# Two fused attention layers on one core: full-bank score pieces, halved output transposes of the last batch, chunk-major x, and a new table of task order

## The chip, the cores and the metric

One core of a Trainium2 chip runs the whole program in one launch. The metric is the device time of that core in microseconds (us), the median of three runs. The engines named below are TensorE (PE, with its weight-load queue PEld), VectorE (DVE), ScalarE (ACT), GpSimd (POOL) and SyncE (SP, which only issues transfers). They run side by side and wait for each other through semaphores.

## The reference

The first layer is a linear attention without softmax, with a norm over each head; the second is a mixture of four small attention experts, two of which count for each token.

```
kv  = einsum('bhsd,bhse->bhde', k, v)          # b=8, h=8, s=576, d=e=64
out = einsum('bhsd,bhde->bhse', q, kv)
x   = out / sqrt(mean(out*out, -1) + 1e-6) * g_norm      # -> (8, 576, 512)

logits = x @ w_gate                             # 4 experts, the best 2 kept
w      = softmax over the 2 kept logits
for e in range(4):
    q, k, v = x @ wq[e], x @ wk[e], x @ wv[e]   # 64 wide each
    a  = softmax(causal(q @ k.T / 8))           # 576 x 576
    y += (w of e, 0 where not kept) * (a @ v @ wo[e])
```

## The kernel before

The work is cut by batch `b` (8 of them), and a batch's 576 tokens by tiles of 128, 128, 128, 128 and 64. The function `graph` lists every piece of work as a task (`("kv", b, c)`, `("x", b, i)` and so on) with its engine, an assumed duration, what it needs and which buffers it holds. The function `plan` walks through these tasks once while the program is built, and takes at each point the ready task with the lowest number from `urgency`, which is worked out from the tables `URGENCY`, `EDGES` and `PERIOD`. The instructions are then emitted in that order, so each engine has a fixed order, and a waiting instruction holds up all that stand behind it on its engine. `SWAP` and `ON_ACT` say whether a PSUM copy runs on ACT or on DVE. `COLD` is the planned time up to which PE's tasks are assumed to take 1.8 times as long.

The stages of a batch, with the task names in brackets:

- SP loads k, v and q. PE forms `p_kv` = k^T v for each head (L567), and copies put it into `kvx` and `kvc` (L454, L456); `p_kt` (L601) and `p_kg` (L611) turn it into four more columns that give the gate logits.
- q is turned by PE for batches 0 and 1 (`p_q`, L585) and by DVE for later ones. `p_out` (L630) is q times `kvx`, five tiles; its copy is `o_sb`, of which there is one buffer.
- ACT squares `o_sb` (L650), DVE sums by head (L656) and takes an inverse root in eleven small steps (L668 to L685).
- POOL multiplies `o_sb` by it and writes `x_tok` (task `xm`, L709), PE turns `x_tok` by four 128-wide transposes a tile (`p_x`, L585), and a copy makes `xT`. The weights' rows are laid out so that chunk `c` of x is every fourth column of `x_tok`.
- PE projects v (L770), q and k (L788) for the four experts, two by two (a pair). Before that POOL multiplies the weights by `g_norm` (task `ws`, L546), out of the same six `x` buffers that `x_tok` uses.
- The scores of a pair (`p_sc`, L814) are made in five pieces (`PIECES`), each in one two-bank PSUM buffer, one bank for each expert of the pair; ACT takes exp of a piece (L828), POOL sets the upper triangle to zero (L834), and PE multiplies by v (`p_pv`, L848).
- DVE scales the result to `osc` (L865 to L876), PE turns it (`p_ot`, L886), a copy makes `OT`, PE multiplies by wo (`p_y`, L896), and SP stores `y`.

PSUM is split into two one-bank buffers (`sm`) and three two-bank buffers (`bg`). The two places in the code that the change of layout and of pieces touches are, before:

```
t = tiles["x", b, i][:].rearrange("p h d -> p (h d)")
transpose_in(i, lambda c: t[:, c : c + NCH * (P - 1) + 1 : NCH], "x", b, i)
...
PIECES = (((0, 0, HALF),), ((0, HALF, S),), ((1, P, S),), ((2, 2 * P, S),), ((3, 3 * P, S), (4, 4 * P, S)))
```

Of the kernel before, what the change touches and what calls it, by code (L numbers as in the profile page):

```python
# [40 lines left out]
def graph(B):  # L41
# [14 lines left out]
    def copy(name, on_act, on_dve, needs, tiles=()):  # L56

        if engine_of(name) == "ACT":
            act(name, on_act, needs, tiles)
        else:  # L60
            dve(name, on_dve, needs, tiles)
# [4 lines left out]
    R5, R4, R2 = range(NB), range(NCH), range(EP)
    for b in range(B):
# [85 lines left out]
        for p in R2:  # L153
            for nm in "qk":
                pe((nm + "p", b, p), 1.12, xT + [("ws", nm, p)], (("bg", nm, b, p),))
            copy(("qpc", b, p), 0.64, 0.78, [("qp", b, p)], (("bg", "q", b, p), ("qTp", b, p)))
            copy(("kpc", b, p), 1.24, 1.50, [("kp", b, p)] + [("sc", b - 1, p, j) for j in R5], (("bg", "k", b, p),))
            hold = (0.31, 0.31, 0.46, 0.34, 0.46)
            took = (0.66, 0.66, 0.95, 0.72, 0.60)
# [2 lines left out]
            for j in R5:
                pe(("sc", b, p, j), hold[j], [("qpc", b, p), ("kpc", b, p)], (("bg", "sc", b, p, j), ("qTp", b, p)))
                act(("exp", b, p, j), took[j], [("sc", b, p, j)] + old, (("bg", "sc", b, p, j),))
                if j != 1:
                    pool(("msk", b, p, j), 0.41 if j < 4 else 0.70, [("exp", b, p, j)])
# [784 lines left out]
```

## Time and profile before

| | |
|---|---|
| median of three runs | 261.76 us (261.53 to 261.89) |
| profiled execution | 259.49 us |
| span of its trace, first to last instruction | 257.8 us |
| mean granted clock of TensorE in it | 0.934 of full speed |
| busy share of the span | PE 89%, PEld 80%, DVE 66%, ACT 59%, POOL 32% |

The profiled execution is one run, and 2.27 us below the median of the timed ones; 1.7 us of it lie outside the span. A busy share is an average over the whole span. In the rows further down, a granted clock of 1.00 is TensorE's upper level (2.4 GHz), and 0.50 its lower one (1.2 GHz).

### The profile page before, as it was taken

Reading aid. Unit: us, or ns where it says so; the run is one execution under the profiler, and the core shown is the slowest. Engines: PE = TensorE matmul, PEld = TensorE weight load, DVE = VectorE, ACT = ScalarE, POOL = GpSimd, SP = SyncE. Lnnn points to the kernel's source line nnn. Section 1 sums busy time; section 2 is a strip of 40 time slices with the busy share of each in tenths; the row PEclk is TensorE's granted clock in tenths of the full one; section 3 lists DMA queues with packets and bytes.
Section 4 is the critical chain, followed back from the end, with each engine's and each line's share of the span. In section 5 each row is a group of like instructions: output and inputs, shape, how many; then the busy total and the mean of one; then the engine's idle time right before and its main releaser. Section 6 shows DMA issues by size and latency. Waiting matters only on the chain.

```text
span 257.8 us, 6403 instructions
## 1 busy us (share of the span) xinstructions
PE 228.5 (89%) x2456; PEld 205.5 (80%) x2456; DVE 169.7 (66%) x503; ACT 152.5 (59%) x277; POOL 82.6 (32%) x160
## 2 busy tenths in 40 slices
PE   0726928999999999999999999989999999999963
PEld 0625826899999989998889889978998999989840
DVE  0085383317986785898688968865858889754560
ACT  0010622176967396449654985699657757976932
POOL 8201725000390038003720183018302730840500
PEclk9977775589999999999999999999999999999995
DMA  6998999999999379999898594131120202123045
GB/s 177 297 160 261 292 222 273 185 145 316 130 163 313 47 143 250 279 155 250 253 140 262 176 188 75 43 122 59 39 88 4 64 0 85 41 65 122 17 170 183
DMA packets 99432, 40.28 MB, mean 156 GB/s; under 512 B 76618, under 2 KB 94538, under 8 KB 99402
## 3 DMA queue, kind: packets, MB, share of 16 engines
q1 hardware_dynamic: 94320, 38.15, 64.0%
q10 hardware_dynamic: 5082, 1.72, 3.0%
q8 instruction: 19, 0.31, 0.6%
q14 instruction: 11, 0.09, 0.1%
HBM read 30.43 MB, written 9.44 MB: 155 GB/s over the span
## 4 chain that ended last, share of the span: by engine, by line
PE 78%; DMA 7%; DVE 6%; ACT 4%; SPq 1%; issue 1%; POOL 0%; DVEq 0%; POOLq 0%; ACTq 0%
PE p_out L630 15%; PE p_sc L814 9%; PE p_x L585 8%; PE p_q L788 7%; PE p_kv L567 7%; PE p_y L896 7%; PE p_v L770 7%; PE p_k L788 7%; PE p_pv L848 5%; DMA q_b<-in_q_dram 3%; DMA k_b<-in_k_dram 3%; ACT PT L828 2%; PE p_ot L886 2%; DMA w_stage<-in_moe_wv_dram 2%; PE p_kg L611 1%
## 5 line engine op out<-in xcount | busy, mean ns | idle before, releaser
L834 POOL TENSOR_SCALAR_AFFINE_SELECT PT<-PT 128x256 bf16<-128x256 bf16 (+1 forms) x80 | 29.3, 384 | 126.1 <-ACT PT L828 125.0
L828 ACT ACTIVATE PT<-p_sc 128x512 bf16<-128x512 f32 (+3 forms) x80 | 50.6, 718 | 3.4 <-PE p_sc L814 3.0
L709 POOL TENSOR_TENSOR x_tok<-o_sb,rs 128x512 f32<-128x512 f32 (+1 forms) x40 | 41.2, 1049 | 19.1 <-DVE rs L685 19.0
L630 PE MATMUL p_out<-kvx,qT 128*128 128x136 f32 x320 | 44.8, 290 | 0.9 <-DVE kvx L456 0.4
L630 PEld LDWEIGHTS p_out<-kvx,qT 128*128 128x128 f32 x320 | 41.2, 197 | 2.3 <-DVE o_sb L456 0.6
L814 PE MATMUL p_sc<-qTp,kT 128*128 128x288 f32 (+4 forms) x192 | 39.0, 323 | 0.0
L656 DVE TENSOR_REDUCE ms<-sq 128x8 f32<-128x520 f32 (+1 forms) x40 | 27.1, 687 | 17.7 <-ACT sq L650 17.2
L585 PE MATMUL p_x<-ident_f,x_tok 128*128 128x128 f32 (+1 forms) x160 | 28.3, 307 | 5.2 <-POOL x_tok L709 4.1
L650 ACT ACTIVATE sq<-o_sb 128x512 f32<-128x512 f32 (+1 forms) x40 | 25.0, 634 | 11.8 <-DVE o_sb L456 9.6
L814 PEld LDWEIGHTS p_sc<-qTp,kT 128*128 128x128 f32 x192 | 28.5, 190 | 3.6 <-ACT PT L828 0.7
L567 PE MATMUL p_kv<-v_b,k_b 128*64 128x64 f32 x512 | 23.4, 242 | 8.9 <-DMA k_b<-in_k_dram 7.8
L567 PEld LDWEIGHTS p_kv<-v_b,k_b 128*64 128x64 f32 x512 | 20.0, 153 | 12.4 <-issue 11.0
L456 DVE COPY o_sb<-p_out 128x544 f32<-128x544 f32 (+1 forms) x30 | 21.4, 716 | 11.2 <-PE p_out L630 11.0
L585 PEld LDWEIGHTS p_x<-ident_f,x_tok 128*128 128x128 f32 (+1 forms) x160 | 23.1, 209 | 7.1 <-POOL x_tok L709 5.5
L770 PE MATMUL p_v<-wv_r,xT 128*128 128x256 f32 x160 | 25.7, 292 | 0.7 <-DVE vext L456 0.7
L896 PE MATMUL p_y<-wo_b,OT 128*128 128x512 bf16 x80 | 23.8, 400 | 1.0 <-ACT OT L454 0.7
L454 ACT CAST kT<-p_k 64x576 fp32r<-64x576 f32 x32 | 20.3, 634 | 4.7 <-PE p_k L788 4.2
L770 PEld LDWEIGHTS p_v<-wv_r,xT 128*128 128x128 f32 x160 | 21.6, 189 | 1.6 <-DVE vext L456 1.1
L788 PE MATMUL p_q<-xT,wq_r 128*128 128x288 f32 x128 | 21.9, 323 | 0.0
L454 ACT CAST xT<-p_x 128x512 fp32r<-128x512 f32 (+1 forms) x25 | 13.3, 545 | 14.3 <-PE p_x L585 14.2
L788 PE MATMUL p_k<-xT,wk_r 128*128 128x288 f32 x128 | 20.2, 303 | 0.0
L788 PEld LDWEIGHTS p_q<-xT,wq_r 128*128 128x128 f32 x128 | 19.3, 206 | 0.3
(86 smaller groups left out, 319.1 us busy)
## 6 DMA issues: line engine op xcount, KB each, us to landing
out_dram<-y SPq DMA_DIRECT2D x32, 256.0 KB, 2.0
k_b<-in_k_dram SPq DMA_DIRECT2D x14, 512.0 KB, 5.2
v_b<-in_v_dram SPq DMA_DIRECT2D x14, 512.0 KB, 7.8
q_b<-in_q_dram SPq DMA_DIRECT2D x48, 144.0 KB, 4.2
q_b<-in_q_dram SPq DMA_DIRECT2D x6, 256.0 KB, 7.5
k_rem<-in_k_dram SPq DMA_DIRECT2D x8, 128.0 KB, 4.3
v_b<-in_v_dram ACTq DMA_DIRECT2D x4, 256.0 KB, 5.3
k_b<-in_k_dram SPq DMA_DIRECT2D x4, 256.0 KB, 6.7
```

What stands on the lines that cost most here:

```text
L454: nc.scalar.copy(dst, src)
L567: nc.tensor.matmul(p_kv[hh * Dh : (hh + 1) * Dh, c, :], lhsT=lhs, rhs=rhs, start=(j == 0), stop=(j == NF), skip_group_check=True,)
L585: nc.tensor.transpose(p_t[:, c, :nt], chunk(c)[:nt], ident_f[:nt, :nt])
L630: nc.tensor.matmul(p_o[:, c // 2, (c % 2) * 256 : (c % 2) * 256 + 2 * GW], lhsT=blocks_of(qT, c)[:, i * P : (i + 1) * P], rhs=kvx[b % 2][: ...
L656: nc.vector.tensor_reduce(mss[b % 2][:nt, i, :], sqs[(NB * b + i) % 3][:nt], axis=AX_X, op=AluOpType.add)
L709: nc.gpsimd.tensor_tensor(out=buf(("x", b, i), [P, H, Dh], FP32, "x_tok")[:nt], in0=ob[:nt, i, :, 0:Dh], in1=st["rstd", b][:nt, i * H : (i ...
L770: nc.tensor.matmul(p_v[:], lhsT=blocks_of(xTs[b % 2], c)[:, i * P : (i + 1) * P], rhs=w_r["v"][:, c, :, :].rearrange("p e f -> p (e f)"), ...
L788: nc.tensor.matmul(p_p[:, s, 0:HALF], lhsT=w_r[nm][:, c, 2 * pr : 2 * pr + 2, :].rearrange("p e f -> p (e f)"), rhs=blocks_of(xTs[b % 2], ...
L814: nc.tensor.matmul(p_s[:, el, o : o + hi - lo], lhsT=kTs[pr][el][:, kb * P : (kb + 1) * P], rhs=tiles["qTp", b, pr][:, lo:hi], start=True, ...
L828: nc.scalar.activation(PT[:, :, d0 : d0 + o], big("sc", b, pr, j)[:, :, 0:o], ACTF.Exp, scale=scale)
L834: nc.gpsimd.affine_select(out=d, in_=d, compare_op=AluOpType.is_ge, fill=0.0, base=0, pattern=[[0, 2], [1, w]], channel_multiplier=-1,)
L896: nc.tensor.matmul(p_y[:], lhsT=blocks_of(OTs[b % 2], pr)[:, qc * P : (qc + 1) * P], rhs=wo_b[:, pr, :], start=(pr == 0), stop=(pr == EP - 1),
```

## The change

1. The scores of a pair are made in four pieces in place of five. The first three hold 512 columns for each expert, which is a full bank, and the fourth holds 64. The matmuls of a pair stay twelve, and their columns stay the same in sum; there is one exp less.
2. `xm` writes `x_tok` with each chunk's 128 columns side by side, so that a transpose reads neighbouring values. The multiplication on POOL then writes four values 512 bytes apart before it goes on to the next four.
3. `p_ot` and its copy are cut in two for the last batch (three tiles, two tiles), and `p_y` of a tile waits only for its half.
4. Which engine does a PSUM copy is chosen task by task, and two of the six `ws` multiplications go from POOL to DVE.
5. `URGENCY`, `EDGES`, `PERIOD` and `COLD` have new numbers, so the order on every engine changes. The function `keep_warm`, which could put idle matmuls on PE, emits none, since `WARM` is 0.

```diff
-ON_ACT = ("kvc", "xc", "qpc", "kpc", "otc", "yc")
-SWAP = {"kgc": (6,), "ktc": (1,), "kvc": (0,), "kvx": (1,), "oc": (0, 1), "otc": (1,), ...
+SWAP = {
+    "ws": (('q', 0), ('v', 0),), "qc": ((0, 4), (1, 0), (1, 1), (1, 3),),
...
+    "kvc": ((1,),), "ktc": ((7,),),
+}
...
-    def copy(kind, b, dst, src):
-        if engine_of((kind, b)) == "ACT":
+    def copy(task, dst, src):
+        if tasks[task][0] == "ACT":
...
-COLD = 15.005
+WARM = 0.0
+COLD = 6.005
-PERIOD = 173.5
+PERIOD = 171.6
...
     def xm(b, i):
         nt = blocks[i][1]
+        shape = [nt, H, Dh // NCH, NCH]
         nc.gpsimd.tensor_tensor(
-            out=buf(("x", b, i), [P, H, Dh], FP32, "x_tok")[:nt],
-            in0=ob[:nt, i, :, 0:Dh],
-            in1=st["rstd", b][:nt, i * H : (i + 1) * H].unsqueeze(2).to_broadcast([nt, H, Dh]),
+            out=buf(("x", b, i), [P, NCH, P], FP32, "x_tok")[:nt].rearrange("p c (h r) -> p h r c", h=H),
+            in0=ob[:nt, i, :, 0:Dh].rearrange("p h (r c) -> p h r c", c=NCH),
+            in1=st["rstd", b][:nt, i * H : (i + 1) * H].unsqueeze(2).unsqueeze(3).to_broadcast(shape),
             op=AluOpType.mult,
         )
     def x_tr(b, i):
-        t = tiles["x", b, i][:].rearrange("p h d -> p (h d)")
-        transpose_in(i, lambda c: t[:, c : c + NCH * (P - 1) + 1 : NCH], "x", b, i)
+        transpose_in(i, lambda c: tiles["x", b, i][:, c, :], "x", b, i)
...
-    PIECES = (((0, 0, HALF),), ((0, HALF, S),), ((1, P, S),), ((2, 2 * P, S),), ((3, 3 * P, S), (4, 4 * P, S)))
+    PIECES = (
+        ((0, 0, NF * P),), ((0, NF * P, S), (1, P, S)), ((2, 2 * P, S), (3, 3 * P, S)), ((4, 4 * P, S),),
+    )
...
-    def ot(b, pr):
-        p_t = small([P, NB * P], "ot", b, pr, dtype=BF16)
-        for qc in range(NB):
+    def ot_part(part):
+        qcs = range(NB) if part is None else GROUPS[part][1]
+        return qcs, qcs[0] * P, min(S, (qcs[-1] + 1) * P)
+
+    def ot(b, pr, part=None):
+        at = (b, pr) if part is None else (b, pr, part)
+        p_t = small([P, NB * P], "ot", *at, dtype=BF16)
+        for qc in ot_part(part)[0]:
```

On PE, the order around the first x transposes (rows 19 to 30 of the program before) was, with `p_kv` of `k_rem_83` and every `p_out` here those of batch 1, and `p_x` and `p_q` out of `xT` those of batch 0:

```order
L585 MATMUL p_x<-ident_f,x_tok 128x128 x8
L567 MATMUL p_kv<-v_b,k_b 64x64 x8
L567 MATMUL p_kv<-v_rem_85,k_rem_83 64x64 x2
L567 MATMUL p_kv<-v_b,k_b 64x64 x8
L567 MATMUL p_kv<-v_rem_85,k_rem_83 64x64 x2
L585 MATMUL p_x<-ident_f,x_tok 128x128 x4
L601 MATMUL p_kt<-ident_f,kvc_89 128x128 x2
L585 MATMUL p_x<-ident_f,x_tok 128x128 x4
L611 MATMUL p_kg<-wg_bd,kvT 128x16 x2
L585 MATMUL p_x<-ident_f,x_tok 128x64 x4
L585 MATMUL p_q<-ident_f,q_b 128x128 x4
L788 MATMUL p_q<-xT_108,wq_r 128x288 x16
```

After the change (rows 22 to 33, all of `p_kv` of batch 1 standing ahead of them) it is:

```order
L625 MATMUL p_q<-ident_f,q_b 128x128 x8
L641 MATMUL p_kt<-ident_f,kvc_89 128x128 x2
L625 MATMUL p_x<-ident_f,x_tok 128x128 x4
L651 MATMUL p_kg<-wg_bd,kvT 128x16 x2
L625 MATMUL p_x<-ident_f,x_tok 128x128 x4
L625 MATMUL p_q<-ident_f,q_b 128x128 x4
L670 MATMUL p_out<-kvx_87,qT 128x136 x4
L625 MATMUL p_x<-ident_f,x_tok 128x128 x4
L670 MATMUL p_out<-kvx_87,qT 128x136 x4
L625 MATMUL p_q<-ident_f,q_b 128x128 x4
L625 MATMUL p_x<-ident_f,x_tok 128x128 x4
L670 MATMUL p_out<-kvx_87,qT 128x136 x4
```

Two q tiles of batch 1 and the second half of its `p_kv` now stand ahead of the first `p_x`; `p_out` of batch 1 stands between the x transposes of batch 0, and the projections follow it, v first.

On SP, the loads after those of batch 0 were:

```order
L540 DMA w_stage<-in_moe_wq_dram 128x2x256 x2
L540 DMA w_stage<-in_moe_wk_dram 128x2x256 x2
L540 DMA w_stage<-in_moe_wv_dram 128x2x256 x2
L555 DMA wo_st<-in_moe_wo_dram 128x512 x2
L493 DMA k_rem_83<-in_k_dram 64x8x64
```

After the change they are:

```order
L593 DMA wo_st<-in_moe_wo_dram 128x512 x2
L530 DMA k_rem_83<-in_k_dram 64x8x64
L530 DMA v_rem_85<-in_v_dram 64x8x64
L518 DMA k_b<-in_k_dram 128x4x256
L518 DMA v_b<-in_v_dram 128x4x256
L518 DMA k_b<-in_k_dram 128x4x256
L518 DMA v_b<-in_v_dram 128x4x256
L542 DMA q_b<-in_q_dram 128x8x64 x4
L542 DMA q_b<-in_q_dram 64x8x64
L577 DMA w_stage<-in_moe_wv_dram 128x2x256 x2
L577 DMA w_stage<-in_moe_wk_dram 128x2x256 x2
```

Six weight loads went behind the k, v and q of batch 1 (the two of wq further still, behind the k and v of batch 2).

On POOL, after the constants, the first rows were:

```order
L546 TENSOR_TENSOR wq_r<-w_stage,g_rows 128x2x4x64 x2
L546 TENSOR_TENSOR wk_r<-w_stage,g_rows 128x2x4x64 x2
L546 TENSOR_TENSOR wv_r<-w_stage,g_rows 128x2x4x64 x2
L709 TENSOR_TENSOR x_tok<-o_sb,rs 128x512 x4
L709 TENSOR_TENSOR x_tok<-o_sb,rs 64x512
```

After the change:

```order
L751 TENSOR_TENSOR x_tok<-o_sb,rs 128x128x4 x4
L584 TENSOR_TENSOR wv_r<-w_stage,g_rows 128x2x4x64
L584 TENSOR_TENSOR wk_r<-w_stage,g_rows 128x2x4x64 x2
L751 TENSOR_TENSOR x_tok<-o_sb,rs 64x128x4
L584 TENSOR_TENSOR wq_r<-w_stage,g_rows 128x2x4x64
```

The weights' multiplications stand behind four of the five `xm` of batch 0, and the fifth behind three of them.

## Rows read from the trace of the kernel before

**Rows 1.** Page, part 1: busy us, share of the span, instructions.

```profile
PE 228.5 (89%) x2456; PEld 205.5 (80%) x2456; DVE 169.7 (66%) x503; ACT 152.5 (59%) x277; POOL 82.6 (32%) x160
```

**Rows 2.** Windows: stretch, busy of PE, PEld, DVE, ACT, POOL, clock, DMA share, GB/s.

```profile
25.80:29.20 3.40, 3.40 (x17) 3.40 (x17) 1.08 (x2) 1.85 (x3) 3.40 (x4) 0.50 1.20 243
29.20:36.05 6.85, 3.82 (x61) 3.51 (x60) 4.45 (x13) 3.71 (x7) 1.70 (x2) 1.00 1.07 284
36.05:53.12 17.07, 13.65 (x87) 11.85 (x88) 6.34 (x24) 2.92 (x7) 5.09 (x5) 0.50 1.05 219
66.00:240.00 174.00, 172.28 (x1909) 157.89 (x1909) 134.80 (x406) 123.11 (x224) 61.08 (x106) 1.00 0.57 130
251.10:257.80 6.70, 2.59 (x6) 0.58 (x5) 0.00 (x0) 2.09 (x4) 0.00 (x0) 0.50 0.50 176
```

**Rows 3.** Waits of PE: total us, times, longest.

```profile
PE p_kv L567 <- DMA k_b<-in_k_dram: 7.8, 2, 7.4
PE p_q L585 <- DVE qT L456: 4.1, 2, 3.7
```

**Rows 4.** Timeline of PE: start, us, what, and the wait ahead of it.

```profile
32.73 0.69 PE L567 MATMUL p_kv<-v_b,k_b 128*64 128x64 f32 x16 [1.09 <-DMA v_b<-in_v_dram]
...
38.19 1.13 PE L585 MATMUL p_x<-ident_f,x_tok 128*128 128x128 f32 x4 [4.08 <-POOL x_tok L709]
```

**Rows 5.** Chain that ended last, 33 to 60 us: start, us, what.

```profile
37.05 1.09 POOL x_tok L709
...
49.29 3.84 PE p_q L788 x16
...
54.06 0.93 PE p_out L630 x8
...
55.82 3.90 PE p_out L630 x32
```

**Rows 6.** The same chain from 160 us on: projections at clock 1.00.

```profile
163.42 2.12 PE p_q L788 x16
```

**Rows 7.** Timeline of SP's issues: start, us, what.

```profile
14.03 3.50 SPq L540 DMA_DIRECT2D w_stage<-in_moe_wq_dram  x2
...
27.49 9.95 SPq L505 DMA_DIRECT2D q_b<-in_q_dram  x5
```

**Rows 8.** Weight loads of transposes of one tile each, at clock 1.00.

```profile
54.71 0.47 PEld L585 LDWEIGHTS p_q<-ident_f,q_b 128*128 128x128 f32 x4
...
55.35 0.32 PEld L585 LDWEIGHTS p_q<-ident_f,q_b 64*128 64x128 f32 x4 [0.17 <-issue]
...
153.43 0.56 PEld L585 LDWEIGHTS p_x<-ident_f,x_tok 128*128 128x128 f32 x4
...
160.33 0.55 PEld L585 LDWEIGHTS p_x<-ident_f,x_tok 64*128 64x128 f32 x4
```

**Rows 9.** Lines by form, POOL: count, busy us, mean ns, idle before.

```profile
L709 POOL TENSOR_TENSOR x_tok<-o_sb,rs 128x512 f32<-128x512 f32 x32 | 33.2, 1052 | 19.1 <-DVE rs L685 19.0
```

**Rows 10.** Lines by form, PE, two of the score matmuls.

```profile
L814 PE MATMUL p_sc<-qTp,kT 128*128 128x288 f32 x64 | 14.6, 325 | 0.0
...
L814 PE MATMUL p_sc<-qTp,kT 128*128 128x64 f32 x32 | 5.2, 246 | 0.0
```

**Rows 11.** Lines by form, ACT, the exps.

```profile
L828 ACT ACTIVATE PT<-p_sc 128x576 bf16<-128x576 f32 x32 | 20.0, 671 | 0.3 <-PE p_sc L814 0.3
L828 ACT ACTIVATE PT<-p_sc 128x896 bf16<-128x896 f32 x16 | 14.9, 932 | 1.0 <-PE p_sc L814 0.8 <-POOL PT L834 0.2
L828 ACT ACTIVATE PT<-p_sc 128x640 bf16<-128x640 f32 x16 | 11.4, 712 | 0.9 <-PE p_sc L814 0.9
L828 ACT ACTIVATE PT<-p_sc 128x512 bf16<-128x512 f32 x16 | 9.7, 605 | 1.2 <-PE p_sc L814 1.1
```

**Rows 12.** Timelines of the tail: DVE, then ACT.

```profile
246.60 0.68 DVE L456 COPY y<-p_y 128x512 f32<-128x512 f32 x1
...
249.04 0.64 ACT L454 COPY OT<-p_ot 128x576 bf16<-128x576 bf16 x1 [0.59 <-PE p_ot L886]
```

More of the change, by code (lines that the diff above doesn't have):

```diff
@@ L54, in dve, with copy @@
         add(name, "DVE", took - 0.05, took + 0.05, needs, tiles)
[L56 to L61, printed above, removed]
     def pool(name, took, needs, tiles=()):
         add(name, "POOL", took - 0.03, took + 0.10, needs, tiles)
+    def copy(name, on_act, on_dve, needs, tiles=(), first=dve):
+        ways = ((dve, on_dve), (act, on_act))
+        if first is act:
+            ways = ways[::-1]
+        make, took = ways[swapped(name)]
+        make(name, took, needs, tiles)
     R5, R4, R2 = range(NB), range(NCH), range(EP)
@@ L94, in graph @@
         copy(("kvx", b), 0.76, 0.84, [("kv", b, c) for c in R4] + [("out", b - 2, i) for i in R5], (("sm", "kv", b),))
-        copy(("kvc", b), 0.37, 0.43, [("kvx", b), ("kt", b - 2)], (("sm", "kv", b),))
+        copy(("kvc", b), 0.37, 0.43, [("kvx", b), ("kt", b - 2)], (("sm", "kv", b),), act)
         for i in R5:
@@ L155, in graph @@
                 pe((nm + "p", b, p), 1.12, xT + [("ws", nm, p)], (("bg", nm, b, p),))
[L156 to L159, printed above, removed]
+            copy(("qpc", b, p), 0.64, 0.78, [("qp", b, p)], (("bg", "q", b, p), ("qTp", b, p)), act)
+            copy(("kpc", b, p), 1.24, 1.50, [("kp", b, p)] + [("sc", b - 1, p, j) for j in R4], (("bg", "k", b, p),), act)
             n = 2 * b + p - 3
             old = [("pv", n // 2, n % 2, g) for g in R2]
[L162 to L166, printed above, removed]
+            for j in R4:
+                pe(
+                    ("sc", b, p, j), (0.47, 0.62, 0.52, 0.24)[j], [("qpc", b, p), ("kpc", b, p)],
+                    (("bg", "sc", b, p, j), ("qTp", b, p)),
+                )
+                act(("exp", b, p, j), 1.09 if j < 3 else 0.28, [("sc", b, p, j)] + old, (("bg", "sc", b, p, j),))
+                pool(("msk", b, p, j), (0.41, 0.41, 0.80, 0.36)[j], [("exp", b, p, j)])
             for g in R2:
-                nd = [("msk", b, p, j) for j in ((0, 2, 3), (0, 2, 3, 4))[g]] + [("exp", b, p, 1)]
+                nd = [("msk", b, p, j) for j in range(3 + g)]
                 pe(("pv", b, p, g), (0.40, 0.58)[g], nd + [("vc", b, i) for i in R5], (("bg", "pv", b, p),))
@@ L351, in buf, with keep_warm @@
             tiles[key] = space.tile(shape, dtype, tag=key[0], name=name, bufs=POOLS[key[0]])
+            if space is psum and dtype == FP32 and len(shape) < 4:
+                t = tiles[key][:]
+                keep_warm(t if len(shape) == 2 else t.rearrange("p a b -> p (a b)"))
         return tiles[key]
+    def keep_warm(t):
+        n = min(512, t.shape[1])
+        for _ in range(int(idle[0] / (n / 2400.0 + 0.01)) if n >= 256 else 0):
+            nc.tensor.matmul(t[:, 0:n], lhsT=zeros[:, 0:P], rhs=zeros[:, 0:n], start=True, stop=True, skip_group_check=True)
+        idle[0] = 0.0
     def big(*key):
@@ L387 @@
     nc.gpsimd.memset(ob[REM:P, NF], 0.0)
+    zeros = const.tile([P, 512], BF16, name="zeros")
+    nc.gpsimd.memset(zeros[:], 0.0)
     zrow = const.tile([P, P], FP32, name="zrow")
@@ L545, in ws @@
     def ws(nm, p):
-        nc.gpsimd.tensor_tensor(
+        eng = nc.gpsimd if tasks["ws", nm, p][0] == "POOL" else nc.vector
+        eng.tensor_tensor(
             out=w_r[nm][:, :, 2 * p : 2 * p + 2, :].rearrange("p c e f -> p e c f"),
@@ L561, in kv @@
     def kv(b, c):
-        p_kv = small([P, NCH, Dh], "kv", b)
+        p_kv = small([P, 2, NCH, Dh], "kv", b)
+        keep_warm(p_kv[:, 1].rearrange("p c d -> p (c d)"))
+        p_kv = p_kv[:, 0]
         for j in range(NF + 1):
@@ L572, in kvx_copy @@
     def kvx_copy(b):
-        p_kv = small(None, "kv", b)
+        p_kv = small(None, "kv", b)[:, 0]
         for hh in range(2):
             pp = slice(hh * Dh, (hh + 1) * Dh)
-            copy("kvx", b, kvx[b % 2][pp, :, hh, 0:Dh], p_kv[pp, :, :])
+            copy(("kvx", b), kvx[b % 2][pp, :, hh, 0:Dh], p_kv[pp, :, :])
     def kvc_copy(b):
-        copy("kvc", b, kvcs[b % 2][:], small(None, "kv", b)[:])
+        copy(("kvc", b), kvcs[b % 2][:], small(None, "kv", b)[:, 0])
     def transpose_in(i, chunk, *key):
@@ L830, in msk @@
     def msk(b, pr, j):
-        for kb, _, _ in PIECES[j]:
+        for kb in ((0,), (1,), (2, 3), (4,))[j]:
             w = blocks[kb][1]
@@ L888, in ot, with ot_copy @@
             )
-    def ot_copy(b, pr):
-        copy("otc", b, OTs[b % 2][:, pr * S : (pr + 1) * S], small(None, "ot", b, pr)[:, 0:S])
+    def ot_copy(b, pr, part=None):
+        at = (b, pr) if part is None else (b, pr, part)
+        _, lo, hi = ot_part(part)
+        copy(("otc",) + at, OTs[b % 2][:, pr * S + lo : pr * S + hi], small(None, "ot", *at)[:, lo:hi])
     def y_mm(b, qc):
```

68 lines of the change are left out of this document (45 added, 23 removed), and 42 rows, old and new, of tables (EDGES, SWAP, URGENCY).

## The prediction, made before the run

> **What bounds the kernel now.** I read the page's busy table first: PE is busy 89% of the span, the next engine 66% [rows 1], so the question is where PE's other 11% lie and whether PE's own work shrinks. The table by windows answers the first part. From 66 to 240 us PE is busy 172.28 of 174.00 us [rows 2]: nothing that only waits less can gain over 1.7 us there, and what counts is PE's own time. Outside that stretch there are two holes. In the start, 29.20 to 53.12 us, PE is first short of work and then runs at the lower level of its clock: it is granted 1.00 up to 36.05, then 0.50 up to 53.12 [rows 2]. At the end, 251.10 to 257.80, it is at 0.50 again and busy for only 2.59 us [rows 2].
>
> The list of PE's waits names what the start waits for: 7.8 us for k by DMA and 4.1 us for the copy of q [rows 3]. PE's own timeline adds the wait that comes last: `p_kv` of batch 1 starts at 32.73, and after it PE stands 4.08 us until the first `x_tok` [rows 4]. That hole is what lies ahead of the fall of the clock at 36.05. The chain of waits shows the price: `xm` at 37.05, then q projections that take 3.84 us for sixteen matmuls [rows 5] where the same sixteen take 2.12 at clock 1.00 [rows 6]. By 59.72 (55.82 + 3.90) PE has done all of x(0), q and `p_out` of batch 1 and the q projections [rows 5]. I call this the mark: the after kernel's gain in the start is how much earlier it has done work of that size.
>
> **The change, part by part.**
>
> *The start.* SP's timeline has the six weight loads first (wq issued at 14.03, 3.50 us for the two) and q of batch 1 only from 27.49 to 37.44 [rows 7]. Taking six loads out of the front brings k, v and q of batch 1 some 4 to 8 us forward, so that `p_kv` of batch 1 and two q tiles fit into the hole ahead of `x_tok`. What bounds the mark then is the chain through `xm`: the first `p_x` is at 38.19 [rows 4]. The copy `kvc` of batch 0 moves from DVE to ACT, and two of the weights' multiplications to DVE; I add 1.2 us to this chain for the former, an estimate from two copies queued ahead of it (0.64 each, the ACT copy of rows 12). Behind the gate, PE's work to the mark at clock 1.00 is: x, four tiles at 0.47 and one at 0.32 (2.2) [rows 8]; three q tiles of the same kind (1.3); `p_out`, five tiles at 0.93 (4.65) [rows 5]; projections of 2.12 [rows 6]; `p_kg`, some 0.2. That is 10.5. I add 2 us of waits: the four further `xm` come 1.05 us apart [rows 9], and the `p_out` between them cover most of that, but a first and a last copy remain. I add 1.7 for the clock: I expect it at 0.50 when `p_x` starts, and price that as one stretch like that from 25.80 to 29.20, 3.40 us in which PE was busy throughout, after which 1.00 was granted; half of it is the loss. The other stretch at 0.50, from 36.05, had gaps and lasted 17.07 [rows 2]. Sum: 38.2 + 1.2 + 10.5 + 2 + 1.7 = 53.6, against 59.72: **a gain of 6.1**. Bounds: with no wait, no delay and the clock at 1.00 all through, 38.2 + 10.5 = 48.7, a gain of 11; with the clock at 0.50 all through, 39.4 + 21 = 60.4, a loss of 0.7. The rest of the program is PE-bound [rows 2], so a shift at the mark reaches the end.
>
> The weights' loads and multiplications are what is late next. They move behind k, v and q on SP and behind four `xm` on POOL. Each writes as many values as an `xm`, so by the same 1.05 us the three behind the fourth `xm` end at 37.05 + 4 x 1.05 + 3 x 1.05 = 44.4 us [rows 5, 9], and the one of wq two places later, at 46.5. `p_out` of batch 1 covers that up to about 46 us, then v, k and q projections come in this order. If the loads came 3 us later than that, it would cost those 3 us; inside the 2 us of waits I count it as met.
>
> *x by chunks.* A transpose's weight load reads `x_tok` at a step of 16 bytes now, and q at a step of 4. Four loads of x take 0.56, of q 0.47; of the 64-token tile 0.55 and 0.32 [rows 8]. So a batch saves 4 x 0.09 + 0.23 = 0.59 by the loads alone. Starts of neighbouring loads are at most as far apart as their own quarter of this, and some are hidden behind the matmul ahead, so I take 0.41, seven tenths. Batch 0 is in the sum of the start, the seven others give **2.9**; bounds 0 (loads hidden) and 7 x 0.59 = 4.1.
>
> The Trainium skill (page "SBUF — State Buffer", section "Specifications (TRN2)", the row on cachelines) says that SBUF has 16-byte lines and that an access wants two hits in a line for its full rate, which agrees with the 0.56 against 0.47 here.
>
> On the other side POOL now writes with a 512-byte step in the innermost loop. No row of before has such a write on POOL. Below, it costs nothing (1.05 stays); above, it costs what a strided access costs at worst in these rows, 0.55 against 0.32 for a 64-token tile [rows 8], a factor of 1.7 and, rounded up, 2: 2.1 us for an `xm`. I take nothing: the 1.05 us for 512 values is far slower than the 0.14 us in which PEld takes a 128-wide step, so the arithmetic sets it and not the access.
>
> A rule of the Trainium skill speaks against this part: the page "GPSIMD Engine Reference", section "7. Performance pitfalls for Q7 kernels", puts about half more time on reads of SBUF whose step is above 8 bytes. It speaks of reads, and the reads here stay side by side; if it held for these writes, an `xm` would take some 1.6 us, an estimate from that page, and forty of them would add 21 us on POOL. No row of before shows it.
>
> *Score pieces.* A pair keeps twelve matmuls and 3200 columns: four of 288 become two of 512 and two of 64. On the line through 64 (246 ns) and 288 (325) a 512 takes 404, and 2 x 404 + 2 x 246 = 4 x 325 [rows 10]: **nothing on PE**, within 1.5 us over sixteen pairs either way, since one change of task fewer and a fuller bank pull in opposite directions. The exps of a pair take 2 x 671 + 932 + 712 + 605 = 3591 ns; on the line through 512 and 896 (0.852 ns an element, 169 fixed) three of 1024 and one of 128 take 3401 [rows 11]. ACT saves 3.0 us in all, behind PE, at 59% busy [rows 1]: nothing on the path.
>
> *The tail.* On DVE a `y` copy of 0.68 stands between the last pair's `osc`, and the last `OT` copy (0.64) is waited for by `p_y` [rows 12]. In halves, the second copy is about half as long, and the `y` copy moves away. I take **0.7**; bounds 0 and 1.3 (both in full).
>
> *Copies by task and the new order in the middle.* With 172.28 of 174.00 us busy [rows 2], there is at most 1.7 to gain, and I take nothing; a worse order could lose several.
>
> **Sum.** Against the profiled execution, 259.5: 259.5 - 6.1 - 2.9 - 0.7 = 249.8. The median of the runs is 2.27 above the profiled one, so 249.8 + 2.3 = **252 us** as a median.
>
> **Rivals.**
>
> *The clock stays low.* PE still has gaps between 30 and 45 us, the projections run at 0.50 as now, and the start gains nothing: 259.5 - 2.9 - 0.7 + 2.3 = 258. For it: now the clock stays at 0.50 for 17.07 us in which PE is busy 13.65 [rows 2]. Against it: `p_kv` and two q tiles fill part of the hole of 4.08.
>
> *Pieces of full banks make PE wait.* Each of the three `bg` buffers is then held for a 1.04 us exp in place of 0.67, with PE ahead by one piece. If a pair costs 0.3 us more, sixteen cost 4.8: 256.8. For it: ACT waits for scores only 0.3 + 1.0 + 0.9 + 1.2 = 3.4 us in all [rows 11], so pieces mostly lie ready for it and hold their buffers. Against it: ACT is 59% busy [rows 1].
>
> *The write step slows `xm`, and the kernel is slower.* At 2.1 us an `xm`, the five of batch 0 add 5.2 in the start, and of 7 x 5.2 in the other batches about half is covered by other work of PE, so 18 more: 252 + 5.2 + 18 = 275. It decides from where the loss eats the 9.7 won: 9.7 / (5 + 17.5) = 0.43 us more an `xm`, 1.48 in all. For it: a new access form that no row prices. Against it: 1.05 us for 512 values is the arithmetic's rate, as I said. By the Trainium skill's rule on GPSIMD's reads, carried over to these writes, the 0.55 us more an `xm` would lie above that point and give some 264 us, an estimate from that page.
>
> *It cancels.* The new order holds PE up in the middle by as much as the rest wins, with time within 0.2% of before.
>
> **Chances.** The forecast's case (start gains 2 or more, the middle as it is) 0.62, on its own 247 to 256; clock low 0.17; full banks 0.10; slower `xm` or an order that loses 0.07; cancelled 0.04. A measurement of this kernel can tell 0.2%, about 0.5 us, from no change. The clock case ends within or above 261.2 in few of its cases, so faster 0.87, same 0.05, slower 0.08. The range 246.5 to 259.5 takes in the first three cases, with the upper bounds of the terms, and leaves out the last two and the start's lower bound.
>
> **What would show it.** Right: in the chain, the first `p_x` near 39 us and the projections' sixteen matmuls nearer 2.1 than 3.8 us; PE's wait for k below 5 us; the mark (q and `p_out` of batch 1, 2.1 us of projections) near 54; PEld's loads of x at 0.47 a tile; `xm` at 1.05; exps of 1024 near 1.04; the stretch after the mark still 99% busy. Wrong: `xm` at 1.5 or more, a clock of 0.50 beyond 48 us, PE waiting in the middle for exps, or a wait for the weights that comes in place of that for k.

## The result, and the profile after

| | before | after |
|---|---|---|
| median of the timed runs | 261.64 us (259.36 to 261.89) | 253.88 us (252.6 to 254.47) |
| profiled execution | 259.49 us | 252.6 us |
| span of the trace | 257.8 us | 250.9 us |
| mean granted clock | 0.934 | 0.977 |

The ratio is 0.9716, with an interval of 0.9649 to 0.9782: the change makes the kernel 7.8 us faster, where 9.7 were forecast (252 us, range 246.5 to 259.5). A second measurement of the same kernel gave 253.52 us and 0.9746 (0.9705 to 0.9787).

The page's busy table of the changed kernel, to be read beside [rows 1]:

```profile
PE 221.2 (88%) x2456; PEld 199.0 (79%) x2456; DVE 180.0 (72%) x510; ACT 148.8 (59%) x258; POOL 81.1 (32%) x159
```

PE is busy for 7.3 us less, almost exactly what the span lost (6.9), so its share stays where it was. A part of this is less work at the clock of 0.50. The windows say where (the columns are those of [rows 2]):

```profile
30.00:37.84 7.84, 5.19 (x100) 4.38 (x99) 7.24 (x23) 3.80 (x7) 0.99 (x1) 1.00 0.98 236
37.84:44.67 6.83, 5.41 (x26) 5.26 (x26) 5.21 (x17) 0.22 (x1) 4.52 (x6) 0.50 1.02 294
70.00:235.00 165.00, 160.06 (x1814) 146.37 (x1812) 130.96 (x374) 113.48 (x197) 53.21 (x94) 0.99 0.59 133
198.27:201.68 3.41, 3.41 (x17) 3.41 (x16) 1.86 (x5) 1.81 (x3) 0.77 (x2) 0.50 0.00 0
241.62:250.90 9.28, 3.85 (x20) 1.44 (x20) 1.44 (x6) 4.41 (x9) 0.00 (x0) 0.92 0.52 185
```

The low stretch in the start is 6.83 us where it was 17.07. In the middle PE now stands 165.00 - 160.06 = 4.94 us; the same 165 us of before had 1.72:

```profile
70.00:235.00 165.00, 163.28 (x1839) 149.04 (x1838) 130.04 (x392) 114.59 (x211) 58.51 (x99) 1.00 0.57 131
```

PE's timeline of the start, as in [rows 4], with the batch-1 `p_kv` and two q tiles (L607, L625) now ahead of the first `p_x`:

```profile
20.43 3.02 PE L625 MATMUL p_q<-ident_f,q_b 128*128 128x128 f32 x12 [5.40 <-ACT kvc L491]
...
26.23 4.90 PE L670 MATMUL p_out<-kvx,qT 128*128 128x136 f32 x40 [0.45 <-DVE kvx L493]
31.06 0.69 PE L607 MATMUL p_kv<-v_b,k_b 128*64 128x64 f32 x16
...
37.51 0.41 PE L641 MATMUL p_kt<-ident_f,kvc 128*128 128x128 f32 x2 [1.78 <-DVE kvc L493]
38.03 1.11 PE L625 MATMUL p_x<-ident_f,x_tok 128*128 128x128 f32 x4
...
41.12 1.09 PE L625 MATMUL p_x<-ident_f,x_tok 128*128 128x128 f32 x4 [1.31 <-DVE xT L493]
```

The wait of 4.08 us ahead of the first `p_x` [rows 4] is gone; what is left are 1.78 and 1.31 us, both for copies on DVE. The chain of waits has the mark:

```profile
51.05 0.93 PE p_out L670 x8
51.98 0.95 PE p_v L811 x8
52.93 1.06 PE p_k L829 x8
...
56.83 2.31 PE p_q L829 x16
```

By 52.93 q and `p_out` of batch 1 and four v tiles (2.30 us in the chain, about the 2.12 of a q projection) are done, so work of the same size as at 59.72 before: 6.8 us earlier. The sixteen q projections take 2.31 us where they took 3.84 [rows 5]. In the profile of the second measurement the same point in the chain comes at 55.01, so 4.7 us earlier than before:

```profile
55.01 1.06 PE p_k L829 x8
```

There the clock is at 0.50 twice in the start, from 27.3 to 30.7 and from 40.9 to 47.7 us, and the first `p_x` comes at 39.58.

### The profile page after: what moved, and what is told of

Its sections match the earlier page's. It is cut to its first block, busy times and chain, and to the rows that moved or that the text cites. A ratio compares the mean times of both kernels' runs of the same rounds, so it can differ in the third digit from the quotient of the medians.

```text
span 250.9 us, 6366 instructions
## 1 busy us (share of the span) xinstructions
PE 221.2 (88%) x2456; PEld 199.0 (79%) x2456; DVE 180.0 (72%) x510; ACT 148.8 (59%) x258; POOL 81.1 (32%) x159
## 3 DMA queue, kind: packets, MB, share of 16 engines
q10 hardware_dynamic: 5082, 1.72, 3.2%
## 4 chain that ended last, share of the span: by engine, by line
PE 71%; DVE 11%; DMA 7%; ACT 7%; issue 1%; SPq 1%; ACTq 0%; DVEq 0%
PE p_out L670 13%; PE p_sc L858 9%; PE p_v L811 8%; PE p_k L829 7%; PE p_q L829 7%; PE p_kv L607 6%; PE p_x L625 6%; PE p_y L948 6%; PE p_pv L892 6%; DMA q_b<-in_q_dram 3%; ACT PT L872 3%; DMA k_b<-in_k_dram 3%; DVE sh L776 2%; PE p_q L625 2%; PE p_ot L936 1%
## 5 line engine op out<-in xcount | busy, mean ns | idle before, releaser
L872 ACT ACTIVATE PT<-p_sc 128x128 bf16<-128x128 f32 (+1 forms) x64 | 51.4, 849 | 6.9 <-PE p_sc L858 6.5
L858 PE MATMUL p_sc<-qTp,kT 128*128 128x64 f32 (+4 forms) x192 | 39.8, 335 | 0.6 <-ACT PT L872 0.4
L607 PE MATMUL p_kv<-v_b,k_b 128*64 128x64 f32 x512 | 21.7, 236 | 7.6 <-DMA k_b<-in_k_dram 7.5
L625 PE MATMUL p_x<-ident_f,x_tok 128*128 128x128 f32 (+1 forms) x160 | 23.4, 279 | 3.9 <-DVE mk L785 2.2
L607 PEld LDWEIGHTS p_kv<-v_b,k_b 128*64 128x64 f32 x512 | 19.3, 148 | 9.4 <-DMA v_b<-in_v_dram 7.3
L948 PE MATMUL p_y<-wo_b,OT 128*128 128x512 bf16 x80 | 22.7, 381 | 1.0 <-ACT xT L491 0.7
L625 PEld LDWEIGHTS p_x<-ident_f,x_tok 128*128 128x128 f32 (+1 forms) x160 | 17.9, 146 | 6.2 <-issue 3.2
L491 ACT CAST xT<-p_x 128x512 fp32r<-128x512 f32 (+1 forms) x30 | 15.7, 546 | 10.6 <-PE p_x L625 10.5
L491 ACT COPY y<-p_y 128x512 f32<-128x512 f32 (+1 forms) x31 | 17.8, 593 | 3.8 <-PE p_y L948 2.6
L829 PE MATMUL p_q<-xT,wq_r 128*128 128x288 f32 x128 | 19.1, 299 | 0.0
L491 ACT CAST kT<-p_k 64x576 fp32r<-64x576 f32 x26 | 16.5, 634 | 4.2 <-PE p_k L829 4.0
```

Source lines behind the costliest of these rows:

```text
L491: nc.scalar.copy(dst, src)
L607: nc.tensor.matmul(p_kv[hh * Dh : (hh + 1) * Dh, c, :], lhsT=lhs, rhs=rhs, start=(j == 0), stop=(j == NF), skip_group_check=True,)
L625: nc.tensor.transpose(p_t[:, c, :nt], chunk(c)[:nt], ident_f[:nt, :nt])
L829: nc.tensor.matmul(p_p[:, s, 0:HALF], lhsT=w_r[nm][:, c, 2 * pr : 2 * pr + 2, :].rearrange("p e f -> p (e f)"), rhs=blocks_of(xTs[b % 2], ...
L858: nc.tensor.matmul(p_s[:, el, o : o + hi - lo], lhsT=kTs[pr][el][:, kb * P : (kb + 1) * P], rhs=tiles["qTp", b, pr][:, lo:hi], start=True, ...
L872: nc.scalar.activation(PT[:, :, d0 : d0 + o], big("sc", b, pr, j)[:, :, 0:o], ACTF.Exp, scale=scale)
```

## Experiments

The ratios are to the kernel before, timed beside it on the same chip; the changed kernel's own is 0.9746 (second measurement). The order of instructions on every engine is that of the kernel named, but for what a diff moves. Experiments 1, 2, 8 and 11 ran on one chip (median of before 260.65 us), 5, 6, 7 and 9 on a second (259.75), 3, 4, 10 and 12 on a third (259.38); across chips the ratios compare better than the medians.

**1. The changed kernel once more (after_again).**

> The changed kernel once more, as the base for the others of this call. Expected within 0.5% of its first result: ratio to before 0.968 to 0.976.

253.52 us, ratio 0.9746. All differences of time below to "the changed kernel" are to this run; where lines of the changed kernel are shown, they are of its first profile unless the text says otherwise.

**2. The rows layout of x_tok back (after_x_rows).**

```diff
-            out=buf(("x", b, i), [P, NCH, P], FP32, "x_tok")[:nt].rearrange("p c (h r) -> p h r c", h=H),
+            out=buf(("x", b, i), [P, H, Dh], FP32, "x_tok")[:nt],
...
-        transpose_in(i, lambda c: tiles["x", b, i][:, c, :], "x", b, i)
+        transpose_in(i, lambda c: t[:, c : c + NCH * (P - 1) + 1 : NCH], "x", b, i)
```

> The changed kernel with x_tok written and read as before (same order on every engine). Theory 1, the prediction's step: the transposes' loads cost PE 0.41 us a batch, and the eight batches show it: 2.6 to 3.3 us slower than the changed kernel, p_x on PE back from about 114 to 132 ns from start to start, and xm back from 1.12 to 1.05 us. Rival: the loads are hidden or the slower xm eats it: within 1 us of the changed kernel.

257.69 us, ratio 0.9904 (0.9868 to 0.994): 4.2 us slower than the changed kernel, with an uncertainty of about 1.4. Lines by form, PEld, of this run (line, count, busy us, mean ns), then of the changed kernel:

```profile
L625 PEld LDWEIGHTS p_x<-ident_f,x_tok 128*128 128x128 f32 x128 | 18.2, 209 | 5.1 <-issue 2.7 <-POOL x_tok L751 1.9
L625 PEld LDWEIGHTS p_x<-ident_f,x_tok 64*128 64x128 f32 x32 | 4.4, 209 | 0.6
```

```profile
L625 PEld LDWEIGHTS p_x<-ident_f,x_tok 128*128 128x128 f32 x128 | 15.3, 148 | 5.6 <-issue 2.8 <-POOL x_tok L751 1.9
L625 PEld LDWEIGHTS p_x<-ident_f,x_tok 64*128 64x128 f32 x32 | 2.6, 138 | 0.7 <-issue 0.3
```

Theory 1's mechanism holds: a load of 64 tokens at a step of 16 bytes costs as much as one of 128, and 61 to 71 ns of each come back. The 4.2 us lie above its 2.6 to 3.3, but within the uncertainty.

**3. x_tok by chunks alone, in the kernel before (before_x_chunks).** The edit is the reverse of that of experiment 2, in the kernel before.

> The kernel before, with x_tok alone written and read by chunks; the order on every engine is that of before. Theory 1: the 4.1 us that the rows layout cost in the changed kernel are mostly PE's own time, so here 2.5 to 4 us below before, p_x at 112 to 115 ns from start to start. Rival: before is bound by other waits, so that under 1 us is seen.

254.83 us, ratio 0.9818 (0.9783 to 0.9853): this part alone gives 4.6 us. From the first `p_x` of batch 1 to the end of the last `p_pv` the profile has 171.9 us (71.0 to 242.9) against 174.6 before (72.5 to 247.1), a gain of 2.7; 1.5 lie ahead of that, in the start. PE's idle time between 70 and 235 us stays small, so the rival falls.

**4. The four score pieces alone, in the kernel before (before_pieces4).**

```diff
-    PIECES = (((0, 0, HALF),), ((0, HALF, S),), ((1, P, S),), ((2, 2 * P, S),), ((3, 3 * P, S), (4, 4 * P, S)))
+    PIECES = (
+        ((0, 0, NF * P),), ((0, NF * P, S), (1, P, S)), ((2, 2 * P, S), (3, 3 * P, S)), ((4, 4 * P, S),),
+    )
...
+        if n[0] in ("sc", "exp", "msk"):        # piece j stands where j + 1 stood
+            if n[0] == "msk" or n[3] == 0: continue
+            new.append(n[:3] + (n[3] - 1,))
+            if n[0] == "exp": new.append(("msk",) + n[1:3] + (n[3] - 1,))
```

> The kernel before, with the four score pieces alone, each in the place of the later piece of before's order. Theory 1, the prediction's step: the same twelve matmuls, so within 1.5 us of before, and 0.7 us more on PE by the rows of after (334 against 335 ns a matmul). Rival, full banks make PE wait for exps of 1.04 us: 3 to 5 us slower than before.

265.11 us, ratio 1.0207 (1.0168 to 1.0246): 5.7 us slower, so this edit is far outside theory 1's 1.5 us. Its window, its waits of PE for `x_tok` in all, and those from 70 to 235 us alone:

```profile
70.00:235.00 165.00, 160.30 (x1769) 144.72 (x1767) 127.44 (x376) 112.33 (x192) 58.63 (x99) 1.00 0.57 127
```

```profile
PE p_x L585 <- POOL x_tok L709: 7.7, 5, 5.1
...
PE p_x L585 <- POOL x_tok L709: 2.6, 4, 1.2
```

PE stands 4.70 us in the 165 where it stood 1.72, and waits for `x_tok` five times where it waited once (4.1 us, in the start); the four new waits, 2.6 us, are most of the 3.0 us more. POOL's timeline has the place: a mask waits for its exp, and `xm` stands behind it. Here, and then the same place before:

```profile
72.33 0.41 POOL L836 TENSOR_SCALAR_AFFINE_SELECT PT<-PT 128x256 bf16<-128x256 bf16 x1 [0.72 <-ACT PT L830]
72.70 1.04 POOL L709 TENSOR_TENSOR x_tok<-o_sb,rs 128x512 f32<-128x512 f32 x1
```

```profile
70.83 0.41 POOL L834 TENSOR_SCALAR_AFFINE_SELECT PT<-PT 128x256 bf16<-128x256 bf16 x1 [0.68 <-ACT PT L828]
71.20 1.11 POOL L709 TENSOR_TENSOR x_tok<-o_sb,rs 128x512 f32<-128x512 f32 x1
72.27 0.40 POOL L834 TENSOR_SCALAR_AFFINE_SELECT PT<-PT 128x256 bf16<-128x256 bf16 x1
```

This order is the edit's own. The kernel before emits a mask 4 to 15 tasks behind its exp; the edit takes every mask from its place and puts it right behind its exp. By that at least one mask more stands ahead of the first `xm` in each of the batches 1 to 5: at 72.33 us it is the one that stood behind that `xm` before (72.27). So the waits for `x_tok` come at least in part from where the masks were put, and not from the PSUM buffers that an exp of 1.04 us holds, as the rival has it. From the start of `p_kv` of batch 2 (59.6 us in both) to the end of the last `p_pv`, 6.1 us are lost: PE stands 3.2 us longer, and is busy for 2.9 us longer with as many matmuls (2109). Which of them take longer was not found. The experiment thus does not price the pieces by themselves. (The 334 ns a matmul in what was expected should be 323, the mean over the score matmuls of before.)

**5. The weight loads ahead again (after_loads_old).**

```diff
+    order = [n for n in order if n not in lw + ws_]
+    at = min(order.index(("lwo", "o", p)) for p in range(EP))
+    order[at:at] = lw               # six weight loads ahead of wo, k, v, q
+    at = order.index(("xm", 0, 0))
+    order[at:at] = ws_              # their multiplications first, all on POOL
```

> The changed kernel with the six weight loads ahead of wo, k, v and q of batch 1 again, and their multiplications first on POOL, as before. Theory 1, the prediction's step: k, v and q of batch 1 come 4 to 8 us later, two q tiles and p_out of batch 1 with them, and the mark moves back by 3 to 6 us. Rival: the chain through the first x_tok at 37 us sets the mark whatever the loads do, and with ready weights the projections wait for nothing: within 1 us of the changed kernel.

258.24 us, ratio 0.9981 (0.994 to 1.0023): 4.7 us slower than the changed kernel by the medians, some 6 us by the ratios. PE's timeline:

```profile
28.89 7.17 PE L670 MATMUL p_out<-kvx,qT 128*128 128x136 f32 x40 [1.67 <-DVE kvx L493]
...
42.16 0.66 PE L625 MATMUL p_q<-ident_f,q_b 128*128 128x128 f32 x4 [3.03 <-DVE kvc L493]
...
43.59 0.89 PE L625 MATMUL p_x<-ident_f,x_tok 128*128 128x128 f32 x4 [0.55 <-ACT qT L491]
```

The first `p_x` comes 5.6 us later than in the changed kernel's first profile (38.03) and 4.0 us later than in its second (39.58): the loads and the weights' multiplications, which this edit moves together, carry most of the start's gain. It is more than the late k and v alone, since `p_out` of batch 0 also started later (28.89 against 26.23). That it took 7.17 us, at 0.50 from 26.7 to 33.6, need not come from the edit: in the changed kernel it took 4.90 us in the first profile and 6.57 in the second.

**6. kvc of batch 0 on DVE (after_kvc_dve).**

```diff
+    tasks["kvc", 0] = ("DVE",) + tuple(tasks["kvc", 0][1:])
```

> The changed kernel with the copy kvc of batch 0 on DVE, as before, so that the second q tile does not wait 5.40 us behind ACT's table load. Theory 1: the wait moves to the next of the chain (wg, kvT), p_out of batch 0 starts up to 1 us earlier and the time falls by 0 to 1.2 us. Rival: PE stands still less at 15 to 20 us but DVE's zeroing is held up instead: within 0.5 us.

255.24 us, ratio 0.9828 (0.9773 to 0.9882): 1.7 us slower by the medians, about 2 us by the ratios, whose intervals overlap a little. The gain of theory 1 did not come; the rival's 0.5 us is not clearly excluded.

```profile
19.25 1.12 PE L625 MATMUL p_q<-ident_f,q_b 128*128 128x128 f32 x4 [3.19 <-DVE qT L493]
...
27.37 6.58 PE L670 MATMUL p_out<-kvx,qT 128*128 128x136 f32 x40 [0.45 <-DVE kvx L493]
```

The wait of 5.40 us for ACT is gone, and three waits for DVE's copies (3.19, 0.79, 0.79) stand in its place; `p_out` starts 1.1 us later. Of this 1.0 us is there already at the first q tile, ahead of these waits (14.94 us against 13.92, behind loads). From the first q tile to `p_out` it is 12.4 us here and 12.3 in the changed kernel: in this place one long wait of PE cost as much as three shorter ones. What makes the kernel slower was not found.

**7. Idle matmuls ahead of the first x tiles (after_dense).**

```diff
+    fill = {("q", 1, 1): 4, ("kt", 1): 8, ("x", 0, 1): 6}
...
+            for _ in range(fill.get(n, 0)):
+                nc.tensor.matmul(big("out", 1, 0)[:, 0, :], lhsT=zeros[:, 0:P], rhs=zeros[:],
+                                 start=True, stop=True, skip_group_check=True)
```

> The changed kernel with 18 idle matmuls of 512 columns on PE in the three waits ahead of the first x tiles (4, 8 and 6). Theory 1: the clock falls to 0.50 at 38 to 41 us because PE stood still for some 3 us ahead of it, so with the gaps filled the low stretch of 6.83 us goes or moves, and the time falls by 1.5 to 3 us. Rival: the x chain through xm and its copies bounds that stretch, or the idle matmuls run over into the work: within 0.7 us or slower.

The six runs went from 249.2 to 255.79 us (median 253.16; the ratio, 0.9641 with 0.956 to 0.9723, is that of the two shortest alone), so the time is unclear. The profiled run (249.2) is clear:

```profile
30.00:37.84 7.84, 7.61 (x109) 5.21 (x109) 7.24 (x26) 3.17 (x6) 1.95 (x2) 1.00 1.04 238
37.84:44.67 6.83, 6.56 (x52) 5.45 (x52) 5.63 (x14) 2.21 (x5) 5.32 (x6) 1.00 1.09 304
```

With PE kept at work the stretch at 0.50 is not there in this execution, and the first `p_x` of batch 1 comes at 58.4 us, 2.8 earlier than in the changed kernel's profile (61.2). The runs in which the time was not less have a lower mean clock (0.952 to 0.957 against 0.996), but only one run has a trace. Experiment 12 has the trace of another kernel with the same idle matmuls.

**8. The gate without sh (after_no_sh).**

```diff
-        nc.scalar.activation(small_t(b, "ex", [P, NB, E]), st["sh", b][:], ACTF.Exp)
+        nc.scalar.activation(small_t(b, "ex", [P, NB, E]), lg8s[b % 2][:, :, 0:E], ACTF.Exp)
```

The reason is this place in the changed kernel, on POOL, DVE and PE:

```profile
191.56 5.07 POOL L751 TENSOR_TENSOR x_tok<-o_sb,rs 128x512 f32<-128x512 f32 x5
```

```profile
193.06 3.93 DVE L776 TENSOR_TENSOR sh<-lg,m 128x20 f32<-128x20 f32 x1
196.92 0.68 DVE L493 CAST xT<-p_x 128x512 fp32r<-128x512 f32 x1
```

```profile
197.74 1.46 PE L625 MATMUL p_x<-ident_f,x_tok 128*128 128x128 f32 x8 [2.17 <-DVE mk L785]
```

A subtraction of 20 values on DVE lasts 3.93 us while POOL works through five `xm`, and ends 0.36 us after the last of them (196.63); a copy to `xT` and then PE stand behind it.

> The changed kernel without the subtraction of the row maximum ahead of the gate's exp (task sh left out; exp reads the logits). Theory 1: in batch 6 that subtraction on DVE lasted 3.93 us because POOL worked through five xm without a gap, and PE waited 2.17 us behind it; without it 2 to 3.5 us faster than the changed kernel. Rival: the next operation with two inputs on DVE (mk or gt) stands there in its place and waits as long: within 0.7 us.

252.48 us, ratio 0.9666 (0.9618 to 0.9714). The median is 1.0 us below the changed kernel's, by the ratios it is 2.1 us, and their intervals overlap: a small gain is likely, and its size is not settled. The trace has the rival's mechanism:

```profile
197.18 2.60 DVE L785 TENSOR_TENSOR mk<-lg,m 128x20 f32<-128x20 f32 x1
```

The next operation of the gate with two inputs lasts 2.60 us in its place.

**9. The gate behind the third x copy (after_gate_late).**

```diff
+    for b in range(B):
+        at = order.index(("xc", b, 2))
+        late = [n for n in [(kind, b) for kind in ("sh", "ex", "mk", "gt", "den", "rd", "gate")] if order.index(n) < at]
+        order = [n for n in order if n not in late]
+        at = order.index(("xc", b, 2)) + 1
+        order[at:at] = late
```

> The changed kernel with the gate's small operations (sh, ex, mk, gt, den, rd, gate) of every batch placed behind the third x copy. Without sh, mk stood there for 2.60 us in its place. Theory 1: what holds DVE is any operation with two inputs while POOL runs its five xm without a gap, so placing them behind takes the waits of batch 5 and 6 away: PE's idle time after 53 us falls from 6.5 to under 4.5 us, time 1.5 to 3 us below the changed kernel (ratio to before near 0.965). Rival: another operation of that kind waits next, or the gate comes late for the scaling of the last tiles: within 0.7 us.

252.79 us, ratio 0.9743 (0.9703 to 0.9783): the changed kernel's ratio.

```profile
70.00:235.00 165.00, 159.96 (x1815) 146.26 (x1825) 128.57 (x382) 114.52 (x198) 53.59 (x94) 1.00 0.60 134
```

The wait of 2.17 us is gone from the trace, and PE still stands 5.04 us in the 165: shorter waits elsewhere add up to the same. Theory 1 named the mechanism of one wait, not the cause of the middle's loss.

**10. The last batch's output transposes whole (after_ot_whole).**

```diff
+    for p in range(EP):
+        for kind in ("ot", "otc"):
+            order.remove((kind, B - 1, p, 0))
+            order[order.index((kind, B - 1, p, 1))] = (kind, B - 1, p)
```

> The changed kernel with the last batch's output transposes whole again (one copy of 576 columns for a pair). Theory 1: 0.4 to 0.8 us slower than the changed kernel, and the time from the end of the last p_pv to the end of the span longer by that. Rival: the fifth y copy waits for a store in both, and the end stays: within 0.3 us.

255.71 us, ratio 0.9846 (0.9805 to 0.9887), about 1% or 2.6 us slower than the changed kernel, more than either theory.

```profile
246.23 0.64 ACT L491 COPY OT<-p_ot 128x576 bf16<-128x576 bf16 x1 [0.93 <-PE p_ot L936]
```

```profile
248.24 2.74 PE L948 MATMUL p_y<-wo_b,OT 128*128 128x512 bf16 x6 [0.23 <-ACT y L491]
```

From the end of the last `p_pv` (244.1) to the end of the span (254.8) it is 10.7 us here, 9.3 in the changed kernel. That is 1.4 us, by the copy's half and by a `p_y` that runs through:

```profile
243.39 3.21 PE L948 MATMUL p_y<-wo_b,OT 128*128 128x512 bf16 x10
```

A part of it can be the clock: in the profile with the whole transposes it is at 0.50 from about 248 to 251 us, in the changed kernel's only in the last 1.5 us. The two were not separated.

**11. Six y buffers (after_y6).** The pool of y tiles gets six buffers in place of four.

> The changed kernel with six y buffers in place of four. Theory: its last y copy waits 2.4 us for a store to give a buffer back, so the end comes 1 to 2 us earlier. Rival: the store that ends last is not that one, or the transfers stand in one queue: within 0.5 us.

254.28 us, ratio 0.976 (0.9718 to 0.9803): no difference to the changed kernel that can be told. In its trace the last five y copies run one behind the other, so the wait for a store was there; but from the end of the last `p_pv` (240.7) to the end of the span (250.0) it is 9.3 us, as in the changed kernel. The end does not hang on that wait, as the rival says.

**12. Idle matmuls and the late gate together (after_dense_gate).**

> The changed kernel with the 18 idle matmuls ahead of the first x tiles and the gate's operations behind the third x copy, together. Theory: with the start at 1.00 as in the profile of the idle matmuls alone (249.2 us) and the wait of batch 6 gone, 248 to 251 us where no low stretch comes elsewhere. Rival: the low stretch comes elsewhere in the start in most runs, and the time is that of the changed kernel less 0.7 us, near 252.8.

251.48 us (249.46 to 253.08), ratio 0.9687 (0.9648 to 0.9727). This is the lowest median of the study, 2.0 us below the changed kernel's, but the intervals of the two ratios overlap: faster than before for certain, faster than the changed kernel not shown. Its trace speaks against the theory. The profiled run is the slowest of the six (253.08), although its mean granted clock is 0.999 and the rows show 0.50 nowhere in its start. One loss in the start is here, where the profile of experiment 7 has 4.90 us for the same forty matmuls, also at 1.00:

```profile
26.78 7.68 PE L670 MATMUL p_out<-kvx,qT 128*128 128x136 f32 x40 [0.45 <-DVE kvx L493]
```

## Why the prediction was right, and where its terms were off

**The start.** Forecast 6.1; the two profiles have 6.8 and 4.7 at the mark, and 4.7 us of time or more come from the order of the weights' loads and multiplications (experiment 5), so the main step holds. The parts came out less well. The first `p_x` was forecast at 39.4 and came at 38.03 and 39.58. `p_out` of batch 0 did start 1.2 us later (26.23 against 25.07), but that this is the price of the copy `kvc` on ACT is not shown: with the copy on DVE the way from the first q tile to `p_out` was no shorter (experiment 6). The low stretch was 6.83 us where 3.4 were put in, and the second profile has 10.2 us at 0.50 in two stretches. That 6.1 lies between the two profiles is in part luck. The rival that the clock stays low and the start gains nothing falls.

**x by chunks.** Forecast 2.9 for seven batches. The trace of experiment 3 has 2.7 for them. The runs give 4.6 alone and 4.2 in the changed kernel for all eight, where the forecast's 0.41 a batch makes 3.3. In the trace of experiment 3 another 1.5 us lie ahead of the first `p_x` of batch 1 (71.0 against 72.5), where batch 0 is turned and where the stretch at 0.50 ends at 47.1 instead of 53.1. So the seven batches came as forecast, and whether the rest is the layout or the clock was not separated. The price of POOL's strided write was forecast at nothing, and nearly is:

```profile
L751 POOL TENSOR_TENSOR x_tok<-o_sb,rs 128x512 f32<-128x512 f32 x32 | 33.6, 1126 | 54.0 <-DVE rs L725 51.5 <-PE p_x L625 2.3
```

That is 1.126 us against 1.052 [rows 9], and five of them take 5.07 us together. The rival that an `xm` doubles falls, and so does the half more that the rule of the Trainium skill (page "GPSIMD Engine Reference", section "7. Performance pitfalls for Q7 kernels") would have given, carried over from reads to these writes.

**Score pieces and the new order in the middle: the terms that were off.** Both were put at nothing. "Nothing on PE" was about right for the matmuls and the exps by themselves; the 192 score matmuls keep PE busy for 39.8 us in place of 39.0:

```profile
L858 PE MATMUL p_sc<-qTp,kT 128*128 128x64 f32 x64 | 12.3, 275 | 0.2 <-ACT kT L491 0.2
L858 PE MATMUL p_sc<-qTp,kT 128*128 128x512 f32 x32 | 11.3, 433 | 0.0
```

```profile
L872 ACT ACTIVATE PT<-p_sc 128x1024 bf16<-128x1024 f32 x48 | 48.4, 1037 | 2.4 <-PE p_sc L858 2.1
```

(404, 1041 and 278 ns were forecast; 433, 1037 and, for the piece of 64, 282 came.) What failed is that the middle as a whole would cost nothing. In the changed kernel the stretch from the mark to the end of the last `p_pv` is 188.7 us (52.93 to 241.62) against 187.4 before (59.72 to 247.1), although x gives 2.7 there: a loss of 4.0. In the second profile it is 187.1 (55.01 to 242.07), a loss of 2.4. Against this stand 3.2 us (second profile 3.4) that PE stands longer in 70 to 235 us, and 1.7 for the low stretch at 198.27, which the second profile does not have; about 1 us less of PE's work, which was not traced, makes up the difference. PE's waits from 70 to 235 us in the changed kernel (total us, times, longest):

```profile
PE p_x L625 <- DVE mk L785: 2.2, 1, 2.2
PE p_v L811 <- DVE vext L493: 0.7, 1, 0.7
PE p_y L948 <- ACT xT L491: 0.7, 1, 0.7
PE p_sc L858 <- ACT PT L872: 0.4, 1, 0.4
```

The largest is that behind the gate's operations on DVE (experiment 8), and 0.6 us in all are for exps. None is for `x_tok`, and the five `xm` of a batch run without a mask between them. So the 3.0 us that PE stands longer in experiment 4 are close to the changed kernel's in size, but they are other waits: the rival of full banks is not shown by them. The waits that are seen hang on what stands ahead of what on DVE, ACT and POOL, so they belong rather to the new order and the copies chosen by task, the last term that was put at nothing. How much of the loss the pieces cause stays open: the changed kernel with the old pieces was not run.

**The tail.** Forecast 0.7, at most 1.3; 10.7 us from the last `p_pv` to the end became 9.3, so 1.4, of which the clock may have a part (experiment 10). In the first profile the differences to the forecast are 0.7 more won in the start and 0.7 in the tail, 0.2 less by x in the seven batches, and 4.0 lost in the middle. They make the 2.8 us between the 249.8 forecast for the profiled run and the 252.6 measured, since the middle is taken as what is left. So the total came near because errors of both signs met, and in the second profile they fall otherwise (1.4 less in the start, 2.4 lost in the middle). The median lies 1.3 us above the profiled run, not 2.3.

## What to carry to other kernels

Before pricing merged pieces at nothing, look at the engine behind them: in experiment 4 a mask that waited for its exp held up an `xm`, and PE waited 2.6 us more for `x_tok`. An edit that is to price one thing must leave the order of the rest as it was; that one did not. Undoing a transposed read on the side of the writer was worth it here: the writer paid 0.07 us an `xm`, and the kernel won 4.2 to 4.6 us. A wait that is removed can come back as its neighbours (experiment 9); count PE's standing time in a stretch, not the wait.
